# One 256 KB block of the Fourier matrix is loaded through ScalarE's queue behind the first activation, and two warm-up products are left out

## The chip, the cores and the metric

The kernel runs on one core of a Trainium2 chip. The core has a matrix engine (TensorE, PE in the profile; its weight loads are PEld), a vector engine (VectorE, DVE), a scalar engine that evaluates functions from tables (ScalarE, ACT), GpSimd (POOL) and SyncE (SP), which here only issues transfers between the device memory and the on-chip memory. Transfers run on 16 DMA engines. SyncE, ScalarE and GpSimd each issue into a queue of their own: q1, q10 and q0 in the profile.

The metric is the device time of one execution in microseconds. The kernel before was run three times: 1025.52, 1025.71 and 1025.87 us, so its median is 1025.71 us and the runs lie within 0.35 us.

## The reference

For an input of 2048 tokens by 640 features, normalised along the features, two branches are added to the input: a Fourier transform over features and tokens of which the real part is kept, written as products with cosine and sine matrices, and a gated linear unit whose gate passes only positive values.

```python
def _A_ref(x, dft_seq_re, dft_seq_im, dft_hid_re, dft_hid_im):
    a = jnp.einsum("bsd,ed->bse", x, dft_hid_re)
    b = jnp.einsum("bsd,ed->bse", x, dft_hid_im)
    y = jnp.einsum("ts,bse->bte", dft_seq_re, a) - jnp.einsum("ts,bse->bte", dft_seq_im, b)
    return y

def _B_ref(x, W_gate, W_up, W_down):
    gate = jnp.einsum("bsd,df->bsf", x, W_gate)
    up = jnp.einsum("bsd,df->bsf", x, W_up)
    gate = gate * (lambda x, dt: x.astype(dt))(gate > 0, gate.dtype)
    h = gate * up
    return jnp.einsum("bsf,fd->bsd", h, W_down)

x = A_x
xn = _layernorm(x, axis=-1)
return x + _A_ref(xn, ...) + _B_ref(xn, B_W_gate, B_W_up, B_W_down)
```

## The kernel before, in words

The work has three phases. The first multiplies the normalised tokens with the 2048 by 2048 token matrices (cosine and sine), streamed from device memory; the second makes the gate and up projections; the third multiplies with the hidden Fourier matrices and the down weights. Every 32-bit operand is split into a rounded high part and a low part, the rest, and each product is made of three (high by high, high by low, low by high), so that one logical block costs three matrix instructions of 128 by 512. A helper makes most splits: ScalarE copies the high part, VectorE or GpSimd subtracts it to give the low part. Recombinations of blocks (sums of quarters of the matrices) reduce the number of products.

This case is about the first ten microseconds. The token matrices are cut into column chunks of 512 (`NCHUNK` = 4) and row blocks of 256 rows, two rows for each of the 128 partitions (`SG` = 2, index `j`). `first_stream(c, name, g)` handles chunk `c` and block `g`; for the first block of chunks 0 and 1 it works in halves of 256 KB, one for each `j`. `st[0]` and `st[1]` are the raw tiles (`raw` in the profile) of chunk 0 and chunk 1. Its `load` issues, in this order, the first 128 tokens in two halves of 160 KB (line 577, the left half through SyncE and the right half through ScalarE), one activation on a one-column tile `root_t` (line 578), whose function makes the compiler put the load of ScalarE's function table in front of it, and then on SyncE: chunk 0 `j` = 0, chunk 1 `j` = 0, the other 128 tokens (320 KB), chunk 0 `j` = 1, chunk 1 `j` = 1 (lines 574 and 198). Tokens appear as `r<-in_x`, matrix blocks as `raw<-in_dft`.

`first_group` then normalises the first tokens and splits the first blocks, in an order that is written out (`pin` keeps the instructions in program order on their engine): statistics on VectorE (lines 203 and 204), an approximate inverse square root on ScalarE (line 209), the rounded normalised tokens on VectorE (line 329), the rounded high part of chunk 0 in two halves (lines 339 and 120, one on each engine), and on ScalarE the mean (212), the centred tokens (334) and then the high part of chunk 1 (line 324). `first_products` (line 540) issues 18 products for `j` = 0 in groups of three, ordered so that what is ready first is used first: the first group takes high tokens and the high part of chunk 0, the second high tokens and the low part of chunk 0, the third the high part of chunk 1, and low tokens and the low part of chunk 1 come later.

Before all this PE runs `WARM` products of 128 by 128 on a constant (line 111), which no result uses.

Later row blocks are loaded by SyncE with 512 KB transfers (line 589) and token groups with 640 KB transfers (line 198), each waiting until its tile is free. Outside the pinned parts a scheduler sets the order of instructions on each engine.

Of the kernel before, what the change touches and what calls it, by code (L numbers as in the profile page):

```python
# [9 lines left out]
AF = mybir.ActivationFunctionType  # L10
OP = mybir.AluOpType

P = 128
S, D, F = 2048, 640, 1728
KD = D // P
CH = 512
# [3 lines left out]
SG = 2  # L20
# [7 lines left out]
NF = F // P  # L28
REST = F - NF * P
EPS = 1e-5  # L30
WARM = 46
BACK = 3


# [24 lines left out]
def fnet_reglu_kernel(  # L59
# [15 lines left out]
    nc = tc.nc  # L75
# [15 lines left out]
    eps_t = keep.tile([P, 1], F32, name="eps_t")  # L91
# [13 lines left out]
    root_t = keep.tile([P, 1], F32, name="root_t")  # L105
# [3 lines left out]
    ps = psum_p.tile([P, CH], F32, name="ps")  # L109
    for i in range(WARM):  # L110
        nc.tensor.matmul(ps[:, :P], warm, warm, start=True, stop=True)  # L111
# [73 lines left out]
    def ln_place(g):  # L185
        if "ln_tile" not in late:
            late["ln_tile"] = get_r1(F32)
        b = g % NH * SG * D
        return late["ln_tile"][:, b : b + SG * D].rearrange("p (j d) -> p j d", j=SG)
# [6 lines left out]
    def ln_load(g, js):  # L196

        return nc.sync.dma_start(ln_place(g)[:, js], x[g * SG * P : (g + 1) * SG * P].rearrange("(p j) d -> p j d", j=SG)[:, js])
# [40 lines left out]
    def pin(steps):  # L239
        return [tc.keep_in_program_order(i) for i in steps]  # L240
# [78 lines left out]
    def first_group(b):  # L319


        xs, bs, mv = ln_tiles(0)
        part = lambda c, j: b[c][1][:, j * CH : (j + 1) * CH]
        high = lambda c, j: pin([nc.scalar.activation(b[c][0][:, 0, j], part(c, j), AF.Copy)])
        low = lambda c, j, engine: pin([engine.tensor_tensor(b[c][0][:, 1, j], part(c, j), b[c][0][:, 0, j].bitcast(F32),
                                                             op=OP.subtract)])
        j0, j1 = slice(0, 1), slice(1, 2)
        def raw_high(j):
            pin([nc.vector.tensor_scalar(ln_parts(0, j, K14)[0], xs[:, j, K14], mv[:, j, 0:1], mv[:, j, 4:5],
                                         op0=OP.subtract, op1=OP.mult)])  # L330

        def center(j):
            pin([ln_mean(0, mv, slice(j, j + 1))])
            pin([nc.scalar.activation(xs[:, j], xs[:, j], AF.Identity, bias=stat[:, 0, 0, j : j + 1])])

        pin(ln_stats(0, xs, bs, mv, j0))
        pin([ln_first(0, mv, j0)])
        for cs, rounded in ((slice(0, HC), copy), (slice(HC, CH), nc.vector.tensor_copy)):
            pin([rounded(b[0][0][:, 0, 0, cs], part(0, 0)[:, cs])])
        raw_high(0)  # L340
        center(0)
        high(1, 0)
        low(0, 0, nc.vector)
        pin(ln_refine(0, mv, j0))
        pin([ln_low(0, xs, 0, K14)])
        pin([nc.vector.memset(b[1][0][:, 1, 0, :1].bitcast(F32), 0.0)])
        low(1, 0, nc.gpsimd)
        pin(ln_stats(0, xs, bs, mv, j1))
        high(0, 1)
        pin([ln_first(0, mv, j1)])  # L350
        raw_high(1)
        high(1, 1)
        center(1)
        pin(ln_refine(0, mv, j1))
        low(0, 1, nc.vector)
        pin([ln_low(0, xs, 1, K14)])
        pin([nc.vector.memset(b[1][0][:, 1, 1, :1].bitcast(F32), 0.0)])
        low(1, 1, nc.gpsimd)
# [85 lines left out]
    def raw():  # L444
        return raw_p.tile([P, W2], F32, name="raw")

    def parts():
        return ring.tile([P, 2, SG, CH], F32R, name="cb")

    def flat(t, v):  # L450
        return t[:, v].rearrange("p j t -> p (j t)")
# [111 lines left out]
    def first_stream(c, name, g):  # L563

        t = {}
        half = int(name == "B21")
        n = half * NH + g

        norm = {0: 0 if n == 0 else None, 1: n + 1 if n < NG - 1 else None}.get(c)

        def load():
            if n == 0 and c == 0:
                st = start["raw"] = [raw(), raw()]
                get = lambda c, j: nc.sync.dma_start(st[c][:, j * CH : (j + 1) * CH], dft[c, 0, 0][:, j * CH : (j + 1) * CH])
                pin([nc.vector.memset(ln_place(0)[:, 0, D - 1 :], 0.0)])
                for queue, cs in ((nc.sync, slice(0, D // 2)), (nc.scalar, slice(D // 2, D))):
                    pin([queue.dma_start(ln_place(0)[:, 0, cs], x[: SG * P].rearrange("(p j) d -> p j d", j=SG)[:, 0, cs])])
                pin([nc.scalar.activation(root_t, eps_t, AF.Abs_reciprocal_sqrt)])
                get(0, 0)
                get(1, 0)  # L580
                ln_load(0, slice(1, 2))
                get(0, 1)
                get(1, 1)
                return
            if norm is not None:
                tc.keep_in_program_order(ln_load(norm, slice(0, SG)))
            if n > 0 or c > 1:
                t["s"] = raw()
                nc.sync.dma_start(t["s"], dft[c, 0, n])
                start[c, n] = t  # L590

        def prepare():
            if norm == 0:
                start["b"] = [(parts(), st) for st in start["raw"]]
                first_group(start["b"])
                return
            if (n > 0 or c > 1) and "b" not in t:
                t["b"] = b = parts()
                with ExitStack() as order:
                    if c == 1:  # L600
                        order.enter_context(tc.issue_after(late["ln"]))
                        order.enter_context(tc.issue_after(late["high"]))
                    i = split(flat(b, 0), flat(b, 1), t["s"])
                if c == 1 and n < NG - 1:
                    late["ln"] = i.ins
                    scale_a21()
            if norm is not None:
                t1 = start[0, norm]
                t1["b"] = parts()
                next_group(norm, t1["b"], t1["s"], flat(b, 1)[:, W2 - 1 : W2] if norm > 1 else None)  # L610

        def run():
            if n == 0 and c < 2:
                first_products(c, start["b"])
                return
            if n > 0 and c == 0:
                next_products(n, t["b"])
                if n == NH - 1:
                    keep_first()
                return  # L620
            accs = [(c, ("e1", i)) for i in range(2)]
            with ExitStack() as order:
                if n > 0 and c == 1:
                    order.enter_context(tc.issue_after(start["pe"]))
                product(g, t["b"], resident(n, 0), accs, half == 0, half == 1, ((c, "v1"), half, half == 0))

        def keep_first():
            t["first"] = sums_a()
            for i, key in enumerate((("e1", 0), ("e1", 1), "v1")):
                pin([copy(t["first"][:, i], E[c, key])])  # L630
            late["finish"]()

        def finish():
            if g == NH - 1:
                s = t.get("first")
                if s is None:
                    s = (sums_a, sums_b)[c % 2]()
                    for i, key in enumerate((("e1", 0), ("e1", 1), "v1")):
                        copy(s[:, i], E[c, key])
                defer(1, lambda: nc.gpsimd.dma_start(pqd[c][0][:, :3] if half else firsts[c], s[:, :3]))  # L640

        todo.append((load, prepare, run, finish))

    def combine(c, name):
# [137 lines left out]
    for step in range(2, SET_STEPS):  # L782
        load, (make, more), halve = token_sets(1, step)
        c, i = 1 + (step - 2) // 2, step % 2
# [331 lines left out]
    def get(q, kind, u):  # L1116
        what, ks = units[u]
        place = (("B22", "B21", "B12", "B11").index(kind) + (q == 0)) % 4
        o = raws[q, kind, u] = (pool("ends").tile([P, 1, CH], F32, name="re") if what == "end" else
                                pool(f"raws{place}").tile([P, 2, CH], F32, name="rw")[:, : len(ks)])  # L1120
        col, row = int(kind in ("B12", "B22")), int(kind in ("B21", "B22"))
        cs = slice(col * CH, (col + 1) * CH)
        if what == "hid":
            nc.sync.dma_start(o, pqd[2 * q + col][row][:, ks[0] : ks[-1] + 1])
        elif what == "end" and row:
            if col:
                nc.gpsimd.memset(o[b2], 0.0)
            nc.sync.dma_start(o[a, 0], hrest[q][:, cs])
        else:
            nc.sync.dma_start(o, hd[q][2 * ks[0] + row : 2 * ks[-1] + row + 1 : 2][:, :, cs].rearrange("f p t -> p f t"))  # L1130
# [232 lines left out]
```

## Time and profile before

| what | value |
|---|---|
| median of three runs | 1025.71 us |
| the profiled execution, its time | 1025.45 us |
| its span, first to last instruction | 1023.6 us |
| products on PE, the 46 warm-up products among them | 4518 |
| PE busy | 1019.0 us |
| VectorE, ScalarE, GpSimd busy | 816.9, 434.1, 123.1 us |
| mean DMA traffic | 243 GB/s |

The time of an execution is 1.85 us longer than the span of its instructions. In the profile a row of the timeline gives the start, the duration, the engine, the line, the instruction with its tiles, and how often it is repeated in a row; a bracket gives the idle time of the engine before it and what ended it. A transfer's row on an issuing engine (SPq, ACTq) gives the time that the issue took, not the transfer; the view of the transfers gives the time from the issue to the landing. "PE busy" counts the modelled overlap of products, so that gaps of PE are read from the distance of starts, or from the chain of work, which goes through PE from 0.79 us to the end.

### The profile page before, as it was taken

Reading aid. Unit: us, or ns where it says so; the run is one execution under the profiler, and the core shown is the slowest. Engines: PE = TensorE matmul, PEld = TensorE weight load, DVE = VectorE, ACT = ScalarE, POOL = GpSimd, SP = SyncE. Lnnn points to the kernel's source line nnn. Section 1 sums busy time; section 2 is a strip of 40 time slices with the busy share of each in tenths; the row PEclk is TensorE's granted clock in tenths of the full one; section 3 lists DMA queues with packets and bytes.
Section 4 is the critical chain, followed back from the end, with each engine's and each line's share of the span. In section 5 each row is a group of like instructions: output and inputs, shape, how many; then the busy total and the mean of one; then the engine's idle time right before and its main releaser. Section 6 shows DMA issues by size and latency. Waiting matters only on the chain.

```text
span 1023.6 us, 12525 instructions
## 1 busy us (share of the span) xinstructions
PE 1019.0 (100%) x4518; PEld 843.8 (82%) x4518; DVE 816.9 (80%) x1102; ACT 434.1 (42%) x553; POOL 123.1 (12%) x193
## 2 busy tenths in 40 slices
PE   9999999999999999999999999999999999999998
PEld 8888888888888888888888888888888888888886
DVE  7957977998989586888878988887696895777983
ACT  5654453443443333433335444444444434544442
POOL 3521001022110001112210000011100000000000
PEclk9999999999999999999999999999999999999999
DMA  8897744968869885555547676674999468896734
GB/s 320 313 300 281 257 128 159 339 224 272 335 231 349 303 320 145 191 193 177 180 143 273 221 247 237 237 274 169 324 396 306 126 240 249 289 326 201 225 99 135
DMA packets 91390, 249.12 MB, mean 243 GB/s; under 512 B 11329, under 2 KB 32385, under 8 KB 88641
## 3 DMA queue, kind: packets, MB, share of 16 engines
q1 hardware_dynamic: 72864, 174.37, 50.0%
q0 software_dynamic: 18176, 73.67, 19.7%
q8 instruction: 35, 0.57, 0.2%
q10 hardware_dynamic: 288, 0.30, 0.1%
q14 instruction: 27, 0.21, 0.1%
HBM read 185.63 MB, written 61.62 MB: 242 GB/s over the span
## 4 chain that ended last, share of the span: by engine, by line
PE 100%; ACT 0%; issue 0%
PE ps L131 31%; PE ps L129 31%; PE ps L130 31%; PE ps L510 3%; PE ps L540 1%; PE ps L1232 1%; PE ps L111 0%; PE ps L1237 0%; ACT y L120 0%
## 5 line engine op out<-in xcount | busy, mean ns | idle before, releaser
L123 ACT ACTIVATE cb<-rw 128x1024 fp32r<-128x1024 f32 x83 | 81.6, 987 | 134.1 <-PE ps L131 87.2
L124 DVE TENSOR_TENSOR cb<-rw,cb 128x1024 fp32r<-128x1024 f32 x83 | 93.7, 1131 | 48.5 <-ACT cb L123 48.2
L123 ACT ACTIVATE cb<-raw 128x1024 fp32r<-128x1024 f32 x71 | 75.2, 1060 | 114.5 <-PE ps L131 106.3
L124 DVE TENSOR_TENSOR cb<-raw,cb 128x1024 fp32r<-128x1024 f32 x71 | 86.8, 1223 | 40.2 <-ACT cb L123 39.8
L129 PE MATMUL ps<-cb,wt 128*128 128x512 f32 x270 | 105.0, 389 | 0.0
L130 PE MATMUL ps<-cb,wt 128*128 128x512 f32 x270 | 105.0, 389 | 0.0
L131 PE MATMUL ps<-cb,wt 128*128 128x512 f32 x270 | 105.0, 389 | 0.0
L129 PE MATMUL ps<-xs_early,gw 128*128 128x512 f32 x260 | 101.2, 389 | 0.0
L131 PE MATMUL ps<-xs_early,gw 128*128 128x512 f32 x260 | 101.2, 389 | 0.0
L130 PE MATMUL ps<-xs_early,gw 128*128 128x512 f32 x260 | 101.1, 389 | 0.0
L120 ACT ACTIVATE gw<-z 128x1024 fp32r<-128x1024 f32 (+1 forms) x52 | 57.7, 1110 | 80.6 <-DVE z L849 79.1
L129 PE MATMUL ps<-cb,xs_late 128*128 128x512 f32 x232 | 90.2, 389 | 0.0
L130 PE MATMUL ps<-cb,xs_late 128*128 128x512 f32 x232 | 90.2, 389 | 0.0
L131 PE MATMUL ps<-cb,xs_late 128*128 128x512 f32 x232 | 90.2, 389 | 0.0
L129 PE MATMUL ps<-cb,xs_early 128*128 128x512 f32 x226 | 87.9, 389 | 0.0
L130 PE MATMUL ps<-cb,xs_early 128*128 128x512 f32 x226 | 87.9, 389 | 0.0
L131 PE MATMUL ps<-cb,xs_early 128*128 128x512 f32 x226 | 87.9, 389 | 0.0
L120 ACT ACTIVATE u<-ps 128x512 f32<-128x512 f32 x52 | 31.1, 597 | 87.6 <-PE ps L131 87.6
L859 DVE TENSOR_TENSOR gw<-z,gw 128x1024 fp32r<-128x1024 f32 (+1 forms) x52 | 64.8, 1284 | 1.3 <-ACT gw L120 1.2
L130 PEld LDWEIGHTS ps<-cb,wt 128*128 128x128 f32 x270 | 50.7, 188 | 10.6
L129 PEld LDWEIGHTS ps<-cb,wt 128*128 128x128 f32 x270 | 50.7, 188 | 10.5
L131 PEld LDWEIGHTS ps<-cb,wt 128*128 128x128 f32 x270 | 50.7, 188 | 10.5
(192 smaller groups left out, 2207.0 us busy)
## 6 DMA issues: line engine op xcount, KB each, us to landing
raw<-in_dft SPq DMA_DIRECT2D x94, 512.0 KB, 5.9
z<-in_wgu SPq DMA_DIRECT2D x26, 640.0 KB, 4.4
wd<-wparts SPq DMA_DIRECT2D x30, 512.0 KB, 5.5
wparts<-pw POOLq DMA_DIRECT2D x12, 1152.0 KB, 5.4
hd<-ob POOLq DMA_DIRECT2D x26, 512.0 KB, 2.9
rw<-hd SPq DMA_DIRECT2D x24, 512.0 KB, 7.3
tk<-in_dft SPq DMA_DIRECT2D x16, 512.0 KB, 6.4
set<-r POOLq DMA_DIRECT2D x16, 512.0 KB, 3.9
```

Source lines behind the costliest of these rows:

```text
L120: return nc.scalar.activation(o, i, AF.Copy)
L123: nc.scalar.activation(hi, src, AF.Copy)
L124: return nc.vector.tensor_tensor(lo, src, hi.bitcast(F32), op=OP.subtract)
L129: nc.tensor.matmul(ps, wh, mh, start=first, stop=False, skip_group_check=more)
L130: nc.tensor.matmul(ps, wh, ml, start=False, stop=False, skip_group_check=more)
L131: nc.tensor.matmul(ps, wl, mh, start=False, stop=last, skip_group_check=more)
L510: start["pe"] = pin([nc.tensor.matmul(E[0, key], xn_part(n * SG + j, d)[v == 1], b[:, int(v == 2), j], start=False, stop=n % NH == NH - 1 ...
L540: pin([nc.tensor.matmul(E[c, key], xn_part(j, d)[v == 1], b[c][0][:, int(v == 2), j], start=j == 0 and v == 0, stop=False)])
L859: tt(self.w[:, 1, cs], self.z[:, cs], self.w[:, 0, cs].bitcast(F32), op=OP.subtract)
L1232: nc.tensor.matmul(B[out], w[:, 0, v, oo : oo + P], b[:, 0, 0], start=False, stop=last and v == 1, skip_group_check=more)
```

## The change

The load of chunk 1 `j` = 0 leaves SyncE's queue. It is issued by ScalarE instead, after the first activation; that activation now writes the first column of the load's own destination `st[1]` in place of `root_t`, so the load, which overwrites the column, has to wait for it. `half` is the ScalarE half of the token load, and `issue_after` keeps the activation behind it. `WARM` goes from 46 to 44.

```diff
-WARM = 46
+WARM = 44
...
-                get = lambda c, j: nc.sync.dma_start(st[c][:, j * CH : (j + 1) * CH], dft[c, 0, 0][:, j * CH : (j + 1) * CH])
+                get = lambda c, j, queue=nc.sync: queue.dma_start(st[c][:, j * CH : (j + 1) * CH], dft[c, 0, 0][:, j * CH : (j + 1) * CH])
                 pin([nc.vector.memset(ln_place(0)[:, 0, D - 1 :], 0.0)])
                 for queue, cs in ((nc.sync, slice(0, D // 2)), (nc.scalar, slice(D // 2, D))):
-                    pin([queue.dma_start(ln_place(0)[:, 0, cs], x[: SG * P].rearrange("(p j) d -> p j d", j=SG)[:, 0, cs])])
-                pin([nc.scalar.activation(root_t, eps_t, AF.Abs_reciprocal_sqrt)])
+                    half, = pin([queue.dma_start(ln_place(0)[:, 0, cs], x[: SG * P].rearrange("(p j) d -> p j d", j=SG)[:, 0, cs])])
                 get(0, 0)
-                get(1, 0)
                 ln_load(0, slice(1, 2))
                 get(0, 1)
                 get(1, 1)
+                with tc.issue_after(half.ins):
+                    nc.scalar.activation(st[1][:, :1], eps_t, AF.Abs_reciprocal_sqrt)
+                get(1, 0, nc.scalar)
                 return
```

On ScalarE the start of the program reads as follows before, where `raw_165` is chunk 0's tile and `raw_166` chunk 1's:

```order
L577 DMA r1_167<-in_x 128x320
L578 ACT_TABLE_LOAD
L578 ACTIVATE root_t_97<-eps_t_77 128x1
L209 ACTIVATE mv_181<-mv_181,eps_t_77 128x1
L120 ACTIVATE cb_178<-raw_165 128x256
L212 ACTIVATE stat_78<-mv_181 128x1
L334 ACTIVATE r1_167<-r1_167,stat_78 128x640
L324 ACTIVATE cb_179<-raw_166 128x512
```

and now, where chunk 0's tile is `raw_163` and chunk 1's is `raw_164`:

```order
L577 DMA r1_165<-in_x 128x320
L583 ACT_TABLE_LOAD
L583 ACTIVATE raw_164<-eps_t_77 128x1
L574 DMA raw_164<-in_dft 128x512
L209 ACTIVATE mv_179<-mv_179,eps_t_77 128x1
L120 ACTIVATE cb_176<-raw_163 128x256
L212 ACTIVATE stat_78<-mv_179 128x1
L334 ACTIVATE r1_165<-r1_165,stat_78 128x640
L324 ACTIVATE cb_177<-raw_164 128x512
```

One transfer stands between the first activation and the inverse square root; the rest keeps its order.

On SyncE the start of the program reads before:

```order
L577 DMA r1_167<-in_x 128x320
L574 DMA raw_165<-in_dft 128x512
L574 DMA raw_166<-in_dft 128x512
L198 DMA r1_167<-in_x 128x640
L574 DMA raw_165<-in_dft 128x512
L574 DMA raw_166<-in_dft 128x512
L198 DMA r1_167<-in_x 128x1280
```

and now:

```order
L577 DMA r1_165<-in_x 128x320
L574 DMA raw_163<-in_dft 128x512
L198 DMA r1_165<-in_x 128x640
L574 DMA raw_163<-in_dft 128x512
L574 DMA raw_164<-in_dft 128x512
L198 DMA r1_165<-in_x 128x1280
```

The second matrix block is gone from the row, and everything behind it stands one place earlier. Further on, two pairs of SyncE's loads change places: a token group (line 198) with the matrix block behind it near 41 us, and a matrix block with the load of a `tk` tile (line 680) behind it near 47 us. On VectorE and GpSimd the order of the instructions is unchanged, and on PE only the two warm-up products are gone.

## The prediction

> **What bounds the kernel now.** I read the page's busy times first, then the chain of work, then the windows, to see whether anything but PE can set the end.
>
> ```profile
> span 1023.6 us, 12525 instructions
> PE 1019.0 (100%) x4518; PEld 843.8 (82%) x4518; DVE 816.9 (80%) x1102; ACT 434.1 (42%) x553; POOL 123.1 (12%) x193
> PE 100%; ACT 0%; issue 0%
> ...
> 0.79 4.92 PE ps L111 x46
> 5.71 8.32 PE ps L540 x36
> 14.04 4.08 PE ps L510 x18
> ...
> 10.00:1019.00 1009.00, 1009.00 (x4452) 835.12 (x4451) 810.92 (x1082) 427.49 (x540) 121.61 (x188) 1.00 0.70 244
> ```
>
> The third group of rows is the chain in its first 20 us: it never leaves PE. Eighteen products of line 510 take 4.08 us, 0.227 us each. Line 540 has 36 products, 8.16 us at that pace, but stands there with 8.32 us: 0.16 us is lost at its start and in one stall. From 10 to 1019 us there are 4452 products, 0.227 us each, so PE has no gap worth naming. The end can move only with the moment the real products begin (5.5 us) and with waits that PE takes afterwards. The change acts on these first eight microseconds, so I read them row by row.
>
> ```profile
> 0.75 0.39 SPq L577 DMA_DIRECT2D r<-in_x  x1
> 0.95 0.38 ACTq L577 DMA_DIRECT2D r<-in_x  x1
> 1.19 0.89 SPq L574 DMA_DIRECT2D raw<-in_dft  x2
> 1.35 1.28 ACT L578 ACT_TABLE_LOAD   x1 [1.35 <-DVE r L575]
> 2.13 0.43 SPq L198 DMA_DIRECT2D r<-in_x  x1
> 2.60 0.92 SPq L574 DMA_DIRECT2D raw<-in_dft  x2
> 2.65 0.20 ACT L578 ACTIVATE root_t<-eps_t 128x1 f32<-128x1 f32 x1
> 3.26 1.00 DVE L203 BATCH_NORM_STATS2 bs<-r 128x6 f32<-128x320 f32 x2 [2.35 <-DMA r<-in_x]
> 4.30 0.21 DVE L204 BATCH_NORM_AGGREGATE mv<-bs 128x2 f32<-128x12 f32 x1
> 4.54 0.29 ACT L209 ACTIVATE mv<-mv,eps_t 128x1 f32<-128x1 f32 x1 [1.69 <-DVE mv L204]
> 4.75 0.40 ACT L120 ACTIVATE cb<-raw 128x256 fp32r<-128x256 f32 x1
> 4.87 0.48 DVE L329 TENSOR_SCALAR xs_early<-r,mv 128x384 fp32r<-128x384 f32 x1
> 5.44 0.83 ACT L334 ACTIVATE r<-r,stat 128x640 f32<-128x640 f32 x1 [0.20 <-ACT stat L212]
> 5.50 1.22 PEld L540 LDWEIGHTS ps<-cb,xs_early 128*128 128x128 f32 x6
> 6.25 0.63 ACT L324 ACTIVATE cb<-raw 128x512 fp32r<-128x512 f32 x1
> 6.94 6.67 PEld L540 LDWEIGHTS ps<-cb,xs_early 128*128 128x128 f32 x30 [0.22 <-ACT cb L324]
> 7.32 1.30 POOL L325 TENSOR_TENSOR cb<-raw,cb 128x512 fp32r<-128x512 f32 x1 [6.86 <-DVE cb L346]
> ```
>
> The first product hangs on the tokens: they land at 3.26, statistics run to 4.51, the inverse square root to 4.83, the rounded tokens (L329) to 5.35, and the first weights are loaded at 5.50. After six products PE waits for the high part of chunk 1 (L324), which ends at 6.88. So L324 is the next thing that can hold PE, and its input is the very block that the change moves.
>
> **The change part by part.** The landings of the transfers concerned come from the transfers' view in narrow windows; the last number of each row is the time from issue to landing. The first five are chunk 0 `j` = 0 (issued 1.19), ScalarE's token half (0.95), the moved block (1.66), the other tokens (2.13) and chunk 1 `j` = 1 (3.08). The sixth is a GpSimd transfer issued at 22.90 beside a busy SyncE queue.
>
> ```profile
> raw<-in_dft SPq DMA_DIRECT2D x1, 256.0 KB, 3.3
> ...
> r<-in_x ACTq DMA_DIRECT2D x1, 160.0 KB, 2.7
> ...
> raw<-in_dft SPq DMA_DIRECT2D x1, 256.0 KB, 4.6
> ...
> r<-in_x SPq DMA_DIRECT2D x1, 320.0 KB, 4.9
> ...
> raw<-in_dft SPq DMA_DIRECT2D x1, 256.0 KB, 5.2
> ...
> xs_early<-st POOLq DMA_DIRECT2D x1, 256.0 KB, 7.0
> ```
>
> So chunk 0 lands at about 4.45, the moved block at 6.25, the other tokens at 7.0 and chunk 1 `j` = 1 at 8.3.
>
> *The issue on ScalarE.* The activation ends at 2.85, so the block is issued at about 2.9 instead of 1.66. An issue occupies ScalarE for about 0.4 us (row 0.95), until 3.3. Behind it stands the inverse square root, which starts at 4.54 when VectorE is done. ScalarE is idle in between, so the issue costs nothing; were the cover gone, 0.4 us would go onto the path of the first product. The activation itself only has another destination of one column: nothing.
>
> *SyncE.* Its later issues come one place, about 0.46 us, earlier. From 2 us on the DMA engines are busy (windows below), so this changes who moves first, not how much moves. The tokens that land at 7.0 are not read by PE before its second half of line 540, and no PE wait hangs on them today: zero.
>
> *The moved block's landing.* This is the term that decides, and the trace has no transfer of this kind on ScalarE's queue beside a full SyncE queue. Low end: ScalarE's token half needed 2.7 us, which gives 2.9 + 2.7 = 5.6. High end: the block lands only after everything that SyncE issued before it, and the same bytes are then done at the same time as today, 8.3. The GpSimd row goes further, 2.9 + 7.0 = 9.9. Between them I count bytes:
>
> ```profile
> 3.00:4.00 1.00, 1.00 (x12) 1.00 (x11) 0.72 (x2) 0.00 (x0) 0.00 (x0) 1.00 0.98 336
> 4.00:5.00 1.00, 1.00 (x12) 1.00 (x10) 0.86 (x4) 0.46 (x2) 0.00 (x0) 1.00 0.88 188
> 5.00:6.00 1.00, 1.00 (x11) 0.96 (x9) 1.00 (x3) 0.80 (x3) 0.00 (x0) 1.00 0.97 335
> ...
> q1 hardware_dynamic: 58, 0.12, 66.1%
> q10 hardware_dynamic: 71, 0.07, 41.0%
> ```
>
> The last number of the window rows is GB/s. The two queue rows are from 2.88 to 3.37 us, when ScalarE's token half met SyncE's matrix block: 58 packets of one and 71 of the other, so the queues share the engines about evenly. If the block begins to move about 1.1 us after its issue, at 4.0, and gets half, its 0.26 MB are through when 0.52 MB have moved: 0.19 by 5.0 and 0.33 by 6.0, so at 6.0. A landing comes later than the bytes' mean, because the slowest of the 16 engines sets it: the other tokens' bytes (160 + 160 + 256 + 256 + 320 KB = 1.18 MB) were counted through at about 6.05 and landed at 7.0. With 0.8 us for that I take 6.8, nearer to the byte count than to either end.
>
> *What PE pays.* ScalarE finishes L334 at 6.27, so L324 cannot start much earlier than its 6.25 of today however early the block lands: a gain is bounded by the 0.07 us or so that PE loses there now. With a landing at 6.8, L324 starts 0.55 us later and PE waits 0.55 us longer. Behind L324 on ScalarE stand the high part of chunk 0 `j` = 1 and the second inverse square root; they and GpSimd's low part (7.32 today, held by VectorE) are read by PE only after the same wait, so they shift with PE and cost nothing a second time.
>
> *The two warm-up products.* 46 of them take 4.92 us, about 0.107 us each, so PE's queue is empty 0.21 us earlier, at about 5.5 instead of 5.7. That is worth something only if the tokens were ready. They are ready at 5.35, and the weights follow a release by 0.05 us (6.88 to 6.94), so 5.40 instead of 5.50 bounds the gain at 0.10 us and zero is the other end. I take 0.03, since an additional semaphore stands before this first load.
>
> *The two exchanged pairs on SyncE.* The loads near 41 us change places:
>
> ```profile
> r<-in_x SPq DMA_DIRECT2D x1, 640.0 KB, 5.1
> ...
> 54.36 0.88 DVE L203 BATCH_NORM_STATS2 bs<-r 128x6 f32<-128x320 f32 x2
> ```
>
> The tokens issued at 40.6 land at 45.7 and are read at 54.36; one 512 KB load ahead of them is covered by 8.6 us. The pair near 47 us is alike: zero.
>
> *Sum.* +0.55 for the wait, −0.03 for the start, about +0.5 us. The profiled execution took 1025.45 us, 0.26 below the median; 1025.95 on its scale, 1026.2 on the median's. A change under 0.2% (2.05 us) is about what a measurement of this kernel cannot tell from no change, so the forecast is "no change", on its slow side.
>
> **The rivals.** *In time.* If the block lands by 6.3, PE waits no more than today and the start may be 0.1 us earlier: 1025.55 to 1025.7. For it: the 2.7 us of ScalarE's token half, and a second queue that is served beside a backlog. Against it: between 4 and 5 us the engines moved only 188 GB/s. [...]
>
> *Behind everything.* The second queue waits until the first has drained what it has. The block lands at 8.3 or later, L324 starts 2.0 us later, PE stalls 2.0 us at its seventh product: 1027.7; by the GpSimd row's 7.0 us, 9.9 and 3.6 us, 1029.3. This decides as soon as the landing passes 8.3. The GpSimd row speaks for it, the even mix against it.
>
> *A slow clock for longer.* The rows of the warm-up products show why they are there:
>
> ```profile
> L111 PEld LDWEIGHTS <-const-bfloat16-1.0 x46: 99/147/147, 0.8 to 5.4; 128*128 128x128 bf16 x46
> L111 PE MATMUL ps<-const-bfloat16-1.0 x46: 219/311/311, 0.8 to 5.5; 128*128 128x128 bf16 x46
> ```
>
> Shortest, median and longest duration: nearly all took 311 ns, only the last ones 219, so PE became faster just before 5.5 us, 4.6 us after its start. If 44 products were too few and as long again were needed, products would take 0.43 us (0.227 × 0.107 / 0.057, the pace of 128 columns before and a quarter of the 512-column pace) for 4.6 us: 10.8 instead of 20.3, 2.2 us lost, 1027.9. Against it: 44 products keep PE busy until about 5.5, past the switch, and real ones follow at once. [...]
>
> **How the numbers follow.** Late by some tenths up to 1.6 us: 0.50, the forecast. In time: 0.32. Behind everything: 0.12, all slower. Slow clock: 0.04, half of it beyond 2.05 us. Something that I do not see, either way: 0.02. Faster by over 0.2% would need the first product 2 us earlier, at 3.5, before the statistics are done: 0.01. That makes 0.01, 0.85 and 0.14. The range goes from 1025.3 (in time, an early start, and the 0.2 us by which runs lie below the median) to 1027.7, the price of the second rival.
>
> **What would show it.** Right: the block's issue on ACTq at about 2.9 and a landing near 6.8; L324 starting then, PEld's bracket at line 540 naming L324 with about 0.8 us; the first real weights at 5.47 to 5.50; line 540's 36 products taking about 8.9 us in the chain. Wrong: a landing before 6.3 with 8.2 us in the chain, a landing after 8.3, warm-up rows that are all 311 ns, or a PE wait after 10 us.

## The result, and the profile after

The changed kernel takes 1027.29 us in the median (19 executions, 1026.78 to 1030.5), the kernel before beside it 1025.71 us (19 executions, 1025.43 to 1026.23): 1.58 us more. The medians alone give a ratio of 1.0015; the ratio over all executions, in which the four longest weigh more, is 1.0018 with a 95% interval of 1.0012 to 1.0025. By the bound of 0.2% that is no change, on its slow side. Fifteen of the 19 lie between 1026.78 and 1027.59; the other four, between 1029.0 and 1030.5, show a mean granted clock (the share of TensorE's full clock that it was given) of 0.998 where the fifteen show 0.999 or 1.0. Two executions at a far lower clock, one of the kernel before (1133.83 us at 0.851) and one of the changed kernel with 46 warm-up products (1326.28 us at 0.728), are left out of all comparisons. The profiled execution took 1026.95 us with a span of 1025.2 us, so it is one of the fifteen; against the profiled execution before it lost 1.50 us.

The busy times, the engines' shares of the chain, the chain through the first microseconds (start, duration, what), and a window over the rest of the span:

```profile
span 1025.2 us, 12520 instructions
PE 1018.4 (99%) x4516; PEld 843.1 (82%) x4516; DVE 817.4 (80%) x1102; ACT 434.7 (42%) x553; POOL 123.0 (12%) x193
PE 99%; DMA 0%; ACT 0%; issue 0%; ACTq 0%; DVE 0%
...
1.35 1.28 ACT L583
...
2.64 0.21 ACT raw L583
...
2.88 4.96 DMA raw<-in_dft
...
7.86 0.64 ACT cb L324
...
8.54 7.10 PE ps L540 x30
15.64 4.08 PE ps L510 x18
...
10.00:1020.00 1010.00, 1010.00 (x4456) 836.25 (x4455) 811.84 (x1086) 429.06 (x540) 121.49 (x188) 1.00 0.70 243
```

Before, the chain was PE alone from 0.79 us on. Now it comes to PE through the table load, the first activation, the moved block (4.96 us from issue to landing) and line 324, and is PE from 8.54 us. Line 510 starts at 15.64 instead of 14.04, 1.60 us later, and the span is 1.6 us longer. The 30 products from the seventh on take 7.10 us here; before, they ran from 6.94 to 14.04, which is 7.10 us too. So the whole loss is made before the seventh product, and nothing is added or given back afterwards: from 10 to 1020 us PE is busy without a gap.

The rows of the timeline around that wait:

```profile
0.79 3.97 PE L111 MATMUL ps<-const-bfloat16-1.0 128*128 128x128 bf16 x44 [0.79 <-PEq L1357]
2.88 0.34 ACTq L574 DMA_DIRECT2D raw<-in_dft  x1
4.62 0.29 ACT L209 ACTIVATE mv<-mv,eps_t 128x1 f32<-128x1 f32 x1 [1.77 <-DVE mv L204]
5.51 0.83 ACT L334 ACTIVATE r<-r,stat 128x640 f32<-128x640 f32 x1 [0.20 <-ACT stat L212]
5.57 1.62 PE L540 MATMUL ps<-cb,xs_early 128*128 128x512 f32 x6 [0.81 <-DVE xs_early L329]
7.86 1.15 ACT L324 ACTIVATE cb<-raw 128x512 fp32r<-128x512 f32 x2 [1.52 <-DMA raw<-in_dft]
8.54 2.14 PEld L540 LDWEIGHTS ps<-cb,xs_early 128*128 128x128 f32 x10 [1.77 <-ACT cb L324]
8.54 2.34 PE L540 MATMUL ps<-cb,xs_early 128*128 128x512 f32 x9 [1.34 <-ACT cb L324]
```

ScalarE is through with line 334 at 6.34 and then idle for 1.52 us until the block lands. PE's first six products start at 5.57; at 0.227 us each, with 0.08 us more for the first, the seventh would start at 7.01 and starts at 8.54: 1.5 us, of which the kernel before paid 0.07.

Why the block needed 4.96 us is in the rows of the two queues. They are for 4 to 5, 5 to 6, 6 to 7 and 7 to 7.9 us; q10 carries nothing but this block then (packets, MB, share of the 16 engines).

```profile
q1 hardware_dynamic: 150, 0.32, 94.9%
q10 hardware_dynamic: 3, 0.01, 1.6%
...
q1 hardware_dynamic: 138, 0.26, 70.3%
q10 hardware_dynamic: 58, 0.12, 30.6%
...
q1 hardware_dynamic: 117, 0.27, 72.7%
q10 hardware_dynamic: 77, 0.13, 33.9%
...
q1 hardware_dynamic: 86, 0.35, 101.7%
q10 hardware_dynamic: 6, 0.01, 2.5%
```

The first packets of the block move just before 5 us, two microseconds after the issue. From then on it has a third of the traffic (0.25 of 0.78 MB in two microseconds), not a half; the last six packets start after 7 us, and the landing follows at 7.84. Chunk 1 `j` = 1, issued 0.3 us ahead of the block on SyncE, lands later still, at about 8.2.

### The profile page after: what moved, and what is told of

Same layout as the page of the kernel before. It is cut to its first block, busy times and chain, and to the rows that moved or that the text cites. A ratio compares the mean times of both kernels' runs of the same rounds, so it can differ in the third digit from the quotient of the medians.

```text
span 1025.2 us, 12520 instructions
## 1 busy us (share of the span) xinstructions
PE 1018.4 (99%) x4516; PEld 843.1 (82%) x4516; DVE 817.4 (80%) x1102; ACT 434.7 (42%) x553; POOL 123.0 (12%) x193
## 4 chain that ended last, share of the span: by engine, by line
PE 99%; DMA 0%; ACT 0%; issue 0%; ACTq 0%; DVE 0%
PE ps L131 31%; PE ps L130 31%; PE ps L129 31%; PE ps L510 3%; PE ps L1233 1%; PE ps L540 1%; DMA raw<-in_dft 0%; PE ps L1238 0%; ACT L583 0%; ACT cb L324 0%; ACT y L120 0%; ACTq L577 0%; ACT raw L583 0%; DVE eps_t L103 0%; DVE r L575 0%
```

## The experiments

The theory was that PE pays, microsecond for microsecond, what the block lands later than it is needed, and that the block lands late because it is issued late. The rivals were the two warm-up products, ScalarE's queue as such, and, for the four executions above 1029 us, a clock that PE loses through its wait.

**Two warm-up products more, on the changed kernel.**

```diff
-WARM = 44
+WARM = 46
```

> The changed kernel with 46 warm-up products again, nothing else. Late-landing theory (PE waits for the moved block, the warm-up products are without weight): the block lands at 7.7 to 8.0 as in the changed kernel, PE waits 1.4 to 1.6 us after its sixth product, 1027.3 us within 0.4. Warm-up theory (two products less leave PE slow or idle and that is the loss): 1025.6 to 1026.0 us, as before the change.

Measured: 1027.07 us in the median of ten executions, ratio to the kernel before 1.0018 (1.0009 to 1.0027). Two executions lie at 1029.28 and 1029.83 with a mean clock of 0.998, eight between 1026.75 and 1027.63. Both groups of the changed kernel are there with 46 warm-up products as well. Where the block landed in these ten is not known: the one profile is of the execution of 1326.28 us, where it lands at 8.82.

**Two warm-up products less, on the kernel before.**

```diff
-WARM = 46
+WARM = 44
```

> The kernel before with 44 warm-up products, nothing else. Late-landing theory: 1025.6 to 1025.9 us, the first real weights at 5.4 to 5.55 us, the first block of the second chunk lands at 6.2 to 6.4. Warm-up theory: 1026.6 us or more.

Measured: 1025.42 us (1025.18 to 1026.35), ratio 1.0000 (0.9991 to 1.0009). That is 0.2 us below the range that I had given, and the warm-up products carry none of the loss. The profiled execution, of 1026.20 us, shows something else: the block does not land at 6.2 to 6.4, as I had expected. Its chain, with the block in its old place on SyncE:

```profile
1.66 5.38 DMA raw<-in_dft
...
7.06 0.64 ACT cb L324
...
7.74 7.10 PE ps L540 x30
```

The same transfer that landed at 6.25 in the profile before lands at 7.04 here, and PE waits 0.78 us. So the landing of this block varies by 0.8 us between executions in which all transfers keep their order. The times of these two kernels lie between 1025.2 and 1026.4, a spread as wide as this; whether the landing makes it is tested below, by the other order on the kernel before.

**The block on ScalarE's queue, issued ahead of the activation** (on the changed kernel; the activation writes its own tile again).

```diff
                 with tc.issue_after(half.ins):
-                    nc.scalar.activation(st[1][:, :1], eps_t, AF.Abs_reciprocal_sqrt)
-                get(1, 0, nc.scalar)
+                    block = get(1, 0, nc.scalar)
+                with tc.issue_after(block.ins):
+                    nc.scalar.activation(root_t, eps_t, AF.Abs_reciprocal_sqrt)
```

> The changed kernel without the hold: the block still goes through ScalarE's queue, but is issued at about 1.35 us, ahead of the function table's load (the activation writes its own tile again). Late-landing theory: what costs is the issue at 2.9; issued 1.5 us earlier the block lands at 5.3 to 6.3 and PE's wait after the sixth product is under 0.2 us, 1025.5 to 1026.0 us, if the first chunk's block is not delayed by sharing (it has 0.2 us to spare). Queue theory (a second queue is served last beside a full first one, whenever it is issued): lands at 7 or later, 1026.5 us or more.

Measured: 1025.47 us, ratio 1.0006 (0.9997 to 1.0015). The block is issued at 1.35 and lands 4.8 us later, at 6.16; the chain is PE alone again:

```profile
0.79 4.78 PE ps L111 x44
5.70 8.46 PE ps L540 x36
```

So ScalarE's queue as such costs nothing in the median. But three of eleven executions took 1027.87 to 1028.62 us, two of them at clock 0.998, and the kernel before stayed below 1026.4; the last two runs come back to that.

**The block last of the five on SyncE** (on the kernel before).

```diff
-                get(1, 0)
                 ln_load(0, slice(1, 2))
                 get(0, 1)
-                get(1, 1)
+                with tc.issue_after(get(1, 1).ins):
+                    get(1, 0)
```

> The kernel before (46 warm-up products, SyncE's queue) with the block issued behind the four other first loads, at about 3.1 us. Late-landing theory with the order of the bytes as the measure: the block lands at 8.2 to 8.4, when the last of the same six transfers landed before, PE waits about 2.0 us, 1027.5 to 1027.9 us. Queue theory: SyncE's queue is the better one, the block lands before the changed kernel's 7.8, under 1027.0 us.

Measured: 1029.70 us (1027.84 to 1029.89), ratio 1.0033 (1.0020 to 1.0046). No ScalarE queue and no hold, only a late issue (3.08), and the loss is larger. The profiled execution, of 1029.73 us; the last three rows are windows, of which the last three numbers are the granted clock, the DMA share and GB/s:

```profile
3.08 5.81 DMA raw<-in_dft
...
8.91 0.64 ACT cb L324
...
9.59 8.60 PE ps L540 x30
...
5.90:9.30 3.40, 1.49 (x6) 0.89 (x5) 2.10 (x9) 0.77 (x2) 0.00 (x0) 1.00 1.01 347
9.40:12.70 3.30, 3.11 (x7) 2.48 (x8) 2.35 (x8) 2.96 (x7) 1.28 (x1) 0.50 1.03 424
12.80:16.00 3.20, 3.20 (x16) 2.60 (x15) 3.13 (x10) 1.36 (x4) 1.30 (x1) 1.00 1.03 423
```

There are two prices here. The block lands at 8.88, half a microsecond later than I had expected, and PE waits 2.4 us. Then, which I had not expected at all, the clock is at half for the window from 9.4 to 12.7: 7 products instead of about 14, so the 30 products take 8.60 us where the changed kernel needs 7.10. The rows on both sides of that window are at 1.00. In the stretch before it PE was busy 1.49 of 3.40 us, so that stretch was not idle: six products ran in it.

**The wait of the changed kernel filled with 24 products on the constant.**

```diff
+FILL = 24
...
                     pin([nc.tensor.matmul(E[c, key], ...)])
+            if j == 0 and (v, cs) == (2, (0,)):
+                for i in range(FILL):
+                    pin([nc.tensor.matmul(ps[:, :P], warm, warm, start=True, stop=True)])
```

> The changed kernel with 24 more constant products of 128 by 128 between PE's sixth and seventh real product, where it waits 1.5 us; at 0.057 us each they take 1.4 us and end before the block is ready. Two-price theory (each execution pays the wait; in about one of four the idle PE also loses its full clock for a while, 2 us more): the median stays at 1026.8 to 1027.4 us, but no run above 1028.5 us and none with a granted clock of 0.998. Rival (the runs above 1029 us are those in which the block lands later still): about one run in four above 1028.5 us as before.

Measured: 1027.10 us, ratio 1.0016 (1.0007 to 1.0025). No execution has a clock below 0.999, nine of eleven lie between 1026.79 and 1027.28, two at 1028.07 and 1028.39. The block lands as late as before (7.85) and the median stays. In the profile PE no longer waits: the useless products fill the time, end 0.2 us after the block's high part is ready (line 540's seventh product starts at 8.72, and could at 8.54), and so cost that much. The executions above 1029 are gone; but if 6 of 29 are long, as in the two runs with this wait unfilled, eleven without one come by chance about once in thirteen times, so the next run has to carry this. What made the two at 1028 is not known; a block that lands a microsecond later would make such a time.

**The same filling, 40 products, with the block last on SyncE.**

```diff
+FILL = 40
...
```

> The kernel with the block last on SyncE's queue (PE waits 2.4 us there, three of five runs at 1029.7 us) with 40 more constant products in the wait, 2.3 us. Two-price theory: all runs between 1027.6 and 1028.4 us, granted clock 0.999 to 1. Rival (late landings): half of the runs at 1029.5 us or more.

Measured: 1028.25 us (1027.73 to 1028.47), ratio 1.0023 (1.0014 to 1.0033), all clocks 0.999 or 1.0, although the block lands as late as without filling, at 9.0. Useless products in the wait take 1.45 us off the median, close to the 1.5 us that the half clock cost in the profile before (8.60 against 7.10). So here the second price is the loss of the clock through PE's idleness, not a later landing. For the four executions of the changed kernel above 1029 us, which were not profiled, this is not the whole account: they lie 2.0 to 3.5 us above the median of the fifteen. A later landing in the same executions would make up the rest; that is not shown.

**The block one place later on SyncE, behind the other tokens** (on the kernel before).

```diff
-                get(1, 0)
-                ln_load(0, slice(1, 2))
-                get(0, 1)
+                with tc.issue_after(ln_load(0, slice(1, 2)).ins):
+                    with tc.issue_after(get(1, 0).ins):
+                        get(0, 1)
```

> The kernel before with the block behind the other tokens on SyncE's queue, one place later, nothing else. Late-landing theory with the order of bytes as measure: lands at 6.9 to 7.8 (the other tokens' landing before), PE waits 0.6 to 1.4 us, 1026.2 to 1027.0 us. Rival (one place does not matter, the 1.2 us of hold and the other queue do): 1025.9 us or less.

Measured: 1026.82 us (1026.26 to 1027.22), ratio 1.0010 (1.0002 to 1.0019). Issued at 2.13, the block lands at 7.29. Here is line 324 in the profiled executions with two warm-up products less on the kernel before, with the block one place later, changed, last on SyncE, and last with filling (line 325 there):

```profile
7.06 0.63 ACT L324 ACTIVATE cb<-raw 128x512 fp32r<-128x512 f32 x1 [0.79 <-DMA raw<-in_dft]
...
7.31 1.28 ACT L324 ACTIVATE cb<-raw 128x512 fp32r<-128x512 f32 x2 [1.13 <-DMA raw<-in_dft]
...
7.86 1.15 ACT L324 ACTIVATE cb<-raw 128x512 fp32r<-128x512 f32 x2 [1.52 <-DMA raw<-in_dft]
...
8.91 1.15 ACT L324 ACTIVATE cb<-raw 128x512 fp32r<-128x512 f32 x2 [2.63 <-DMA raw<-in_dft]
...
9.05 1.15 ACT L325 ACTIVATE cb<-raw 128x512 fp32r<-128x512 f32 x2 [2.75 <-DMA raw<-in_dft]
```

| profiled execution | line 324 later than before (6.25) | its time over before's 1025.45 |
|---|---|---|
| 44 warm-up products only | 0.81 | 0.75 |
| block one place later | 1.06 | 1.07 |
| changed kernel | 1.61 | 1.50 |
| block last on SyncE, filled | 2.80 | 2.78 |
| block last on SyncE | 2.66 | 4.28 |

One microsecond of landing is one microsecond of time, to 0.1 us, whichever queue issued the block; only the row in which PE lost its clock stands out, by 1.6 us.

The profiles say one thing more, which the prediction could have used. From its issue to its landing the block needs 4.6 to 5.4 us in its first place on SyncE, 5.2 one place later, 5.8 and 5.9 in the last place, 5.0 to 5.2 on ScalarE's queue when held, and 4.8 to 5.6 there when not held. That is at most 1.3 us of difference, of which an unchanged place alone makes 0.8. A held load needs no longer than one that is not held: the hold costs by its later issue, and not by a slower transfer.

**Another order of PE's first products, on the changed kernel:** the three products of low tokens by the high part of chunk 0 come ahead of those that need chunk 1.

```diff
-        for v, cs in (((0, (0,)), (2, (0,)), (0, (1,)), (1, (0, 1)), (2, (1,))),
+        for v, cs in (((0, (0,)), (2, (0,)), (1, (0,)), (0, (1,)), (1, (1,)), (2, (1,))),
```

> The changed kernel with PE's products in another order: the three that need low tokens and the first chunk's high part come before the ones that need the block, so PE needs the block 0.68 us later. The low tokens are ready at 7.2. Late-landing theory: the first needed input makes PE wait 0.2 us, the block the rest, together 0.8 to 0.9 instead of 1.5: 1026.4 to 1026.9 us as median. Rival (the loss does not hang on this wait): 1027.0 to 1027.4 us as before.

Measured: 1026.72 us (1026.10 to 1027.44), ratio 1.0011 (1.0002 to 1.0020), no clock below 0.999. In the profiled execution the block lands at 8.04; PE waits 0.25 us for the low tokens and 0.73 us for the block, 1.0 instead of 1.5 us, although the block is 0.2 us later. A later need is worth as much as an earlier landing, less what the products drawn ahead wait for.

**The same order on the kernel before.**

> The kernel before, with only the order of PE's first products changed: the three products of low tokens by the high part of chunk 0 come ahead of those that need chunk 1. The moved block stays where it was, on SyncE, and lands at 6.2 to 7.0. By the theory that PE pays the landing less the moment at which it first needs the block, a landing of 7.0 no longer costs 0.78 us: the block is needed 0.7 us later. In its place PE takes a wait for the low tokens of about 0.25 us (as in the run with the other order on the changed kernel), in every execution. So the lower runs stay at 1025.4 to 1025.7 and the higher group near 1026.0 to 1026.4 goes: median 1025.5 to 1025.7, no difference that can be measured against the kernel before. Rival: the wait for the block is not what makes the higher group of the kernel before; then the spread stays 1025.3 to 1026.4 and the median rises by the 0.25 us of the new wait to 1025.9.

Measured: 1025.88 us (1025.75 to 1026.05, eleven executions), ratio 1.0002 (0.9993 to 1.0011); the kernel before beside it 1025.60 (1025.37 to 1026.14). The spread shrinks from 0.77 to 0.30 us, as the theory has it; but the median is 0.28 us up, above the range that I had given and where the rival had it. In the profile the sixth product starts at 6.66 and the seventh at 7.12, 0.23 us late, because it waits for the low tokens; the lowest execution is 0.38 us up, which fits a wait that is paid every time. The order removes the variation and gains nothing.

**The activation writes its own tile, the load only stands behind it in ScalarE's order** (on the changed kernel).

```diff
                 with tc.issue_after(half.ins):
-                    nc.scalar.activation(st[1][:, :1], eps_t, AF.Abs_reciprocal_sqrt)
-                get(1, 0, nc.scalar)
+                    first = nc.scalar.activation(root_t, eps_t, AF.Abs_reciprocal_sqrt)
+                with tc.issue_after(first.ins):
+                    get(1, 0, nc.scalar)
```

> The changed kernel, but the first activation writes its own one-column tile again, so the block's load has no data to wait for; it only stands behind that activation in ScalarE's queue. The table load (1.28 us) runs from 1.35 in any case. By the theory that the place in ScalarE's order makes the load late, the issue comes right behind the activation's start, at 2.65 to 2.9 instead of 2.88, the block lands at 7.6 to 7.9, PE waits 1.3 to 1.55 us at its seventh product, and the median is 1027.0 to 1027.3, the changed kernel's. Rival: it is the wait on the activation's result that holds the load; without it the load is issued at about 1.4, while the table load runs, lands at about 6.2, and the median is 1025.4 to 1025.8, that of the run in which the load stood ahead of the activation.

Measured: 1025.65 us, nine of eleven executions between 1025.20 and 1026.15, two at 1026.83 and 1028.21; ratio 1.0002 (0.9993 to 1.0012). My theory fell and the rival holds: ScalarE's start in the profiled execution reads

```profile
1.36 1.28 ACT L583 ACT_TABLE_LOAD   x1 [1.36 <-DVE r L575]
1.42 0.39 ACTq L574 DMA_DIRECT2D raw<-in_dft  x1
2.65 0.20 ACT L583 ACTIVATE root_t<-eps_t 128x1 f32<-128x1 f32 x1
```

The load stands behind the activation in the program's order, and is issued at 1.42 while the table load runs, before the activation. It lands at 6.98 here, later than the rival said, inside the spread seen on SyncE (6.25 to 7.04). Standing behind the table load and the activation delays the issue by 0.07 us (1.35 in the run with the load ahead of them); what moves it to 2.88 is the wait for the one column that the activation writes. SyncE's row of loads is the same as in the changed kernel, so what SyncE issues earlier is not the loss either. In the median, that column is the whole loss of the changed kernel.

**That kernel with the later need of chunk 1** (both edits as above), to find what its few long executions come from.

> The kernel of the run before this (block on ScalarE's queue, not held by the first activation), with the other order of PE's first products, so that the block is needed about 0.7 us later. In the two runs with the block early on ScalarE's queue, 5 of 22 executions were above 1026.5, which the kernel before never was. Theory: in those executions the block landed late, at 7.5 or beyond, and PE waited long enough to lose its clock now and then. Then the later need takes 0.5 to 0.7 us off each, none has a mean clock of 0.998 and none is above 1027.5; the others pay the 0.25 us for the low tokens: median 1025.7 to 1025.9. Rival: the tail does not come from the block (the first tokens or the first moment of the full clock, for example); then it stays as it is, with one to four of 11 executions above 1027.5.

Measured: 1025.90 us, ratio 1.0006 (0.9997 to 1.0015), with four of eleven executions between 1026.63 and 1027.87, one of them at clock 0.998. The tail stays, so the block's landing is not its only cause: here too the rival holds. It is shorter than in the two runs before (at most 2.0 us above the median, there 2.6 and 3.2), so that a part of it may still be the landing. The profiled execution is one of the four (1026.63 us):

```profile
1.20 4.27 DMA raw<-in_dft
...
5.49 0.29 DVE L339 CAST cb<-raw 128x256 fp32r<-128x256 f32 x1 [0.69 <-DMA raw<-in_dft]
5.70 0.47 DVE L329 TENSOR_SCALAR xs_early<-r,mv 128x384 fp32r<-128x384 f32 x1
6.32 0.94 PE L540 MATMUL ps<-cb,xs_early 128*128 128x512 f32 x3 [1.49 <-DVE xs_early L329]
```

Now chunk 0 `j` = 0, issued at 1.20 on SyncE, is late: it lands at 5.47. In the profile before it landed at about 4.45, in the changed kernel at 4.40, in the other two with the block early at 4.59 and 4.85. VectorE takes its rounded half (line 339) ahead of the tokens (line 329), so PE's first product comes at 6.32 instead of 5.5. About 0.3 us of that is not chunk 0: the first tokens land later too, and the inverse square root (line 209) starts at 4.83 instead of 4.54. In the profile of the load that stands behind the activation in order alone, it is the first tokens that are late: VectorE has to wait for their right half, which stands on ScalarE's queue just ahead of the block:

```profile
3.97 0.49 DVE L203 BATCH_NORM_STATS2 bs<-r 128x6 f32<-128x320 f32 x1 [0.23 <-DMA r<-in_x]
```

In the three profiles with the block early on ScalarE's queue the first product started at 5.69, 5.70 and 6.32, in the ten others between 5.42 and 5.62. On SyncE's queue the block stood behind the first tokens and chunk 0; early on another queue it competes with them. From issue to landing the first tokens' half on ScalarE's queue needs 2.8, 2.9 and 3.0 us in these three profiles and chunk 0 `j` = 0 3.7, 3.4 and 4.3 us, against 2.7 and 3.3 us in the profile before. The profiles show this for moderate cases; the executions beyond 1027.8 were not profiled, so that the same thing makes them is likely, not shown.

## Why the prediction was right, and where it was not

The forecast was "no change, on its slow side", for the right reason: PE waits at its seventh product for the high part of chunk 1. The time lies in the range, but 1.1 us above the value, and one step of the sum has all of it. That the range still holds it is partly luck: its upper end, 1027.7, is the price of a rival that fell, and four of the 19 executions lie above it. The 1.58 us are also at the very edge of what the forecast called "late by some tenths up to 1.6 us".

- **PE alone sets the end: right.** Line 324 starts 1.61 us later, line 510 1.60 us later, the span is 1.6 us longer.
- **The issue on ScalarE costs nothing: right.** It is at 2.88 and takes 0.34 us; the inverse square root behind it still waits for VectorE (1.77 us in its bracket). That the activation's other destination costs "nothing" was true of the instruction alone: the wait that it makes is the 1.46 us between an issue at 1.42 and one at 2.88.
- **SyncE's earlier issues cost nothing on the path: right, but they were not idle.** The other tokens landed at 6.1 instead of 7.0. Part of the bytes that moved ahead of the block were theirs.
- **The moved block's landing: the step that failed.** I put it at 6.8, and it was 7.84. Two inputs of the byte count were off. I let the block begin 1.1 us after its issue; beside a full SyncE queue it began two microseconds after it, at about 5.0. And I gave it half of the traffic, from half a microsecond in which two transfers met, counted in packets; it got a third. In bytes those two rows said it already: 0.07 of 0.19 MB. A shorter way stood in the prediction's list of landings: SyncE's loads behind the first needed 4.6, 4.9 and 5.2 us from the issue, which from 2.9 gives 7.5 to 8.1. The margin of 0.8 us for the slowest engine was right: 138 of the 144 packets are in the rows up to 7.0, and the landing came 0.84 later. The trace has 16 signals for each of these landings; the block's run from 6.49 to 7.84, and those of the other tokens in the profile before from 5.72 to 7.01. With 7.84 in the sum the wait grows by 1.59 instead of 0.55 us, and the sum is 1025.45 + 1.59 − 0.03 = 1027.0, against 1026.95 measured.
- **The wait's own price: right per microsecond, incomplete.** The table above gives one for one. That a wait can also cost the full clock I had tied only to missing warm-up products; four of 19 executions show the lower mean clock (0.998) and are 2.0 to 3.5 us longer.
- **The warm-up products: right, nothing.** 46 on the changed kernel and 44 on the kernel before change neither. But "PE's queue is empty at about 5.5" is not a fixed moment: the 44 products ended at 4.76 in the profile after, at 4.70 on the kernel before, at 4.83 in the last run, and at 5.43 to 5.64 in four other profiles, depending on when the distance of their starts fell from 0.107 to 0.06 us.
- **The exchanged loads on SyncE: right, nothing.** There is no gap on PE from 10 us on.
- **The rivals.** *In time* fell: it needed a landing by 6.3, and the block landed at 7.84. In the trace's records of single packets its 128 packets of 2 KB, most of them 0.084 us long, start between 4.94 and 7.35 us. The rival's time is what the kernel gives when the load is not held. *Behind everything* fell by half a microsecond: the block landed before 8.3, ahead of chunk 1 `j` = 1, and shared the engines (0.25 of the 0.78 MB from 5 to 7 us were its own), but was nearer to this end than to the value I took. When really last on SyncE, it lands at 8.88. *A slow clock for longer* fell as put, by the two runs with the other number of warm-up products; the half clock came by another way.

## What to carry to other kernels

A load that is held by an instruction's result is issued late, and lands later for it: here it was issued 1.53 us later and landed 1.68 us later than with the load ahead of the activation, and 1.46 and 0.86 us later than with the load behind it in order alone. To forecast the landing, take the time from issue to landing of loads of its size in the same stretch of the trace (here 4.6 to 5.9 us in every place and queue) before any even split of the traffic, and look at what first waits for it. Moving a load to another queue also takes away the order in which it stood behind more urgent ones: here that delayed the first product by 0.1 to 0.8 us in three profiles, and is the one thing the hold was good for. Where PE must wait early in the kernel, useless products in the wait can keep its clock: with a wait of 2.4 us in the profile three of five executions were at 0.998 and none of ten with the wait filled; with one of 1.5 us six of 29, and none of eleven with it filled. With waits of about 1 us, unfilled, none of 22 was below 0.999. Too many such products end behind the input and cost time themselves (24 ended 0.2 us behind it here).

## What the runs showed of the hardware that I had not expected

- A transfer that stands behind a table load and an activation in ScalarE's order is issued 0.06 us after the table load starts (1.42 after 1.36), if it depends on neither.
- The same transfer in the same place landed at 6.25 and at 7.04 us in two executions, a spread of 0.8 us, which is more than the whole difference between several of these kernels.
- In one profiled execution PE lost half its clock for about 3.3 us after a stretch of 3.4 us in which it still ran six products (1.49 us busy). With 40 useless products in that wait none of ten executions has a clock below 0.999, where three of five had 0.998.
- The moment from which PE's products ran at full pace differs between executions: the steps between the starts of the constant products fall from 0.107 to 0.06 us at about 3.5 us in the profile after and at about 5.4 in the profile before, although the first product starts at 0.79 in both.
